# Softplus in one ScalarE instruction: a changed activation in the second layer of an attention and two-layer MLP kernel

## The chip, the cores and the metric

The kernel runs on one core of one Trainium2 chip. Its engines have queues of their own and wait for each other by semaphores: TensorE (PE, matmuls into PSUM; PEld is its weight load), VectorE (DVE), ScalarE (ACT), GpSimd (POOL) and SyncE (SP, which issues the transfers). The metric is the device time of one execution, in microseconds. The kernel before takes 1000.08 us, the median of three runs (998.30, 1000.08 and 1001.85).

## The reference, cut to what matters

Masked attention gives x (2304 tokens by 512), layer 1 is a gated unit behind an RMS norm, and layer 2, which the change touches, is an MLP with a softplus:

```python
def _moe2_ref(x, w_in, w_out):            # x (2304, 512), w_in (512, 2048), w_out (2048, 512)
    h = x @ w_in
    g = np.maximum(h, 0.0) + np.log1p(np.exp(-np.abs(h)))
    return (g @ w_out).astype(np.float32)
```

The weights arrive as 64-bit floats.

## The kernel before, in words

Every matmul operand is held as two parts, a rounded high part and the rest as a low part (xh and xl, gh and gl, and the two halves of each weight buffer). `mm3` (L255) does a product in three matmuls: high by high, high by low, low by high (L261).

The tokens lie in five chunks (`CUTS`: four of 512 and one of 256). Layer 1 has 12 blocks of 128 features, layer 2 has 16; a block is called f, and two of them make a group. There are four weight buffers (wa, w1, w2, w3; block f has the one of number f % 4), so the weights of the next group are read and split while the present group runs. `split` (L227) takes one tile of 512 columns: a DMA on SP, Abs on ScalarE that reads the upper words (L240), the sign mask (L241) and the assembly (L243) on VectorE, the rounding by a Copy on ScalarE (L246), two more steps on VectorE (L247, L249) and two on GpSimd (L252, L253). Its scratch tiles cvt, cvu and cvr exist once, so the next tile's Abs waits for L253 of the tile before. A block of layer 2 has two such tiles.

In layer 2 one block and one chunk go so: `project` gives h (128 features by the chunk's tokens) in one PSUM bank by 12 matmuls; `chain2` (L560) makes the softplus of h and splits it into gh and gl; `out2` (L581) multiplies them by the output weights, six matmuls of 512 columns for each 128 tokens and pair of blocks, and VectorE adds the bank to acc (L601; L599 the first time). The loop at L691 asks for the projections and chains of both blocks for chunk c, and only then for `out2` of chunk c-1. TensorE takes its matmuls in just this order; `out1` of layer 1's last chunk comes after the first projections of layer 2.

The other engines' order is not that of the text. `Program.emit` (L73) plans the whole of both layers with a cost for each operation (the helpers at L176 to L189) and a due time that follows from when TensorE needs the result; each engine takes, of what is ready by the plan, what is due first. The order is then fixed: on the chip every engine works its queue in order and waits at its head.

Activation functions come from table sets. The program loads one by name with `table` (L188), and an instruction that is marked as needing the table stays behind that load; Abs and Copy are not marked. One load stands ahead of layer 2 (L673), for the set that has Exp and Ln.

`chain2` takes three scratch tiles from the ring "ri" of six (four quarters of ssq, which layer 1 has no more use for, and two gv tiles), and a gh and a gl tile, of which there are four each.

Of the kernel before, what the change touches and what calls it, by code (L numbers as in the profile page):

```python
# [13 lines left out]
AF = mybir.ActivationFunctionType  # L14
ALU = mybir.AluOpType
AX = mybir.AxisListType
EXP_LN = "natural_log_exp_and_others"
# [25 lines left out]


class Program:
    """Instructions in program order, with what each reads and writes. emit() gives every
    engine a queue in which no instruction waits long while a later one could run. TensorE
    takes its main stream in program order, and the side stream where that one would wait."""

    def __init__(self):  # L50
        self.nodes, self.seen, self.ends = [], {}, []
# [103 lines left out]
def attn_glu_softplus(  # L155
# [14 lines left out]
    nc = tc.nc  # L170
    pr = Program()

    def all_of(key):
        return (key, 0, 1 << 30)

    def dve(n, fn, r, w, fast=False):  # L176
        pr.add("DVE", 69 + n / (1.92 if fast else 0.96), fn, r, w)

    def act(n, fn, r, w, table=False):
        pr.add("ACT", 93 + n / 1.2, fn, r + ([all_of("table")] if table else []), w)  # L180

    def pool(n, fn, r, w):
        pr.add("POOL", 110 + n * 2.2, fn, r, w)

    def dma(kb, fn, r, w):
        pr.add("SP", 650, fn, r, w, lag=1800 + 6 * kb)

    def table(name):  # L188
        pr.add("ACT", 1300, lambda: nc.scalar.preload_act_table_set(name), [], [all_of("table")])  # L189
# [10 lines left out]
    def ring(pool_, name, n, shape, dt=F32):  # L200
        return Ring([pool_.tile(shape, dt, name=f"{name}{i}") for i in range(n)], name)
# [18 lines left out]
    fk = {"gv": ring(const, "gv", 1, [128, CH]), "gh": ring(const, "gh", 2, [128, CH], F32R),  # L220
          "gl": ring(const, "gl", 2, [128, CH], F32R)}
# [288 lines left out]
    def project(f, o, c, ring_):  # L510
        pb, kb_ = ring_.next()
        pairs = []
        for kk, mv in enumerate(xs_of(c)):
            rx = [cols("xh", kk, CUTS[c], CUTS[c + 1]), cols("xl", kk, CUTS[c], CUTS[c + 1])]
            rw = wreg(f, o + kk * 128, 128)
            pairs.append((w_of(f, o + kk * 128), mv, lambda a, b, rx=rx, rw=rw: [rw[a], rx[b]]))
        n = CUTS[c + 1] - CUTS[c]
        pb = pb[:, :n]
        mm3(pb, kb_, pairs, n)
        return pb, kb_  # L520
# [39 lines left out]
    def chain2(f, c, hb, fk):  # L560
        h, kp = hb
        n = CUTS[c + 1] - CUTS[c]
        (e, ke), (l, kl), (t, kt) = (fk["ri"].next() for _ in range(3))
        e, l, t = e[:, :n], l[:, :n], t[:, :n]
        act(n, lambda: nc.scalar.activation(e, h, AF.Abs), [kp], [ke])  # L565
        act(n, lambda: nc.scalar.activation(e, e, AF.Exp, scale=-1.0), [ke], [ke], True)
        act(n, lambda: nc.scalar.activation(l, e, AF.Ln, bias=1.0), [ke], [kl], True)
        dve(n, lambda: nc.vector.tensor_scalar(out=t, in0=e, scalar1=1.0, scalar2=1.0,  # L568
                                               op0=ALU.add, op1=ALU.subtract), [ke], [kt], True)
        pool(n, lambda: nc.gpsimd.tensor_sub(t, e, t), [ke, kt], [kt])  # L570
        pool(n, lambda: nc.gpsimd.tensor_add(l, l, t), [kl, kt], [kl])  # L571
        dve(n, lambda: nc.vector.scalar_tensor_tensor(out=l, in0=h, scalar=0.0, in1=l,  # L572
                                                      op0=ALU.max, op1=ALU.add), [kp, kl], [kl])
        sh, kh = fk["gh"].next()
        sl, ksl = fk["gl"].next()
        sh, sl = sh[:, :n], sl[:, :n]
        dve(n, lambda: nc.vector.tensor_copy(sh, l), [kl], [kh], True)  # L577
        dve(n, lambda: nc.vector.tensor_sub(sl, l, sh.bitcast(F32)), [kl, kh], [ksl])  # L578
        return f, (sh, sl), (kh, ksl)

# [25 lines left out]
    def weights(f, wpool):  # L606
        w_t[f] = (wpool, f"w{f % 4}")
        for s in range(3 if f < W1N else 2):
            split(wpool, f"w{f % 4}", f, s)

    with tc.manual_schedule():
        table(EXP_LN)
        pr.add("DVE", 200, lambda: nc.vector.memset(ones, -1.0 / DM), [], [all_of("ones")])
        pr.add("DVE", 100, lambda: nc.vector.memset(eps, 1e-6), [], [all_of("eps")])
        pr.add("DVE", 100, lambda: nc.vector.memset(lnc, math.log(RC)), [], [all_of("eps")])
        wa = const.tile([128, 2, 1536], F32R, name="wa")
        first = {}

        plan = {}

        def at_step(u, fn, *args):
            plan.setdefault(u, []).append((fn, args))

        at_step(8, weights, 0, wa)
        g0 = {}

        def half(c, o):
            first[c, o] = project(0, o, c, f_banks)

        def glu(c):  # L630
            table("silu_and_others")
            g0[c] = chain1(0, c, first[c, 0], first[c, 512], fk)
            table(EXP_LN)

        for c, u in enumerate(START):
            at_step(u, stats, c, f_banks)
            at_step(u + 2, half, c, 0)
            at_step(u + 3, half, c, 512)
            if c < 2:
                at_step(u + 4, glu, c)  # L640

        def fill(u):
            pr.side = True
            for fn, args in plan.pop(u, ()):
                fn(*args)
            pr.side = False

        dma(96, lambda: nc.sync.dma_start(out=pat[64:128], in_=mk), [], [all_of("pat")])
        dma(64, lambda: nc.sync.dma_start(out=id_sb, in_=ident), [], [all_of("id")])
        dma(2, lambda: nc.sync.dma_start(out=rg_sb, in_=rg), [], [all_of("rg")])  # L650
        for i in range(WARM):
            pr.add("PE", 400, lambda: nc.tensor.matmul(
                f_banks.t[0][:, :128], lhsT=ones, rhs=ones, start=True, stop=True), [all_of("ones")], [("bank6", 0, 128)])
        at_stack = ExitStack()
        attention(at_stack, fill)
        pr.emit()
        at_stack.close()
        wb = ctx.enter_context(tc.tile_pool(name="wb", bufs=1))
        acc = wb.tile([128, KD * NT], F32, name="acc")
        acc_t = acc.rearrange("p (k t) -> p k t", k=KD)  # L660
        acc_o = acc.rearrange("p (i n) -> p i n", n=DM)
        wts = [wa] + [wb.tile([128, 2, 1536], F32R, name=f"w{i}") for i in range(1, 4)]
        for key, dt in (("gv", F32), ("gh", F32R), ("gl", F32R)):
            for i in range(EXTRA[key]):
                fk[key].t.append(wb.tile([128, CH], dt, name=f"{key}x{i}"))
        fk["ri"] = Ring([ssq[:, i * CH:(i + 1) * CH] for i in range(NT // CH)] + fk["gv"].t, "ri")
        todo = []
        for gi, fs in enumerate(groups):
            for f in fs:
                if f:  # L670
                    weights(f, wts[f % 4])
            if gi == len(G1):
                table(EXP_LN)  # L673
            if gi == 0:
                out1(0, 0, [g0[0]])
                stats(3, banks)
                stats(4, banks)
                banks.k += 2
                table("silu_and_others")
                gate, val = first[2, 0], first[2, 512]  # L680
                for c in range(2, NCH):
                    todo.append((out1, 0, c, [chain1(0, c, gate, val, fk)]))
                    if c < NCH - 1:
                        gate, val = project(0, 0, c + 1, banks), project(0, 512, c + 1, banks)
                    if c == 2:
                        out1(0, 1, [g0[1]])
                    elif c > 2:
                        fn, *args = todo.pop(0)
                        fn(*args)
                continue  # L690
            for c in range(NCH):  # L691
                if gi < len(G1):
                    gt = [chain1(f, c, project(f, 0, c, banks), project(f, 512, c, banks), fk) for f in fs]
                    todo.append((out1, gi, c, gt))
                else:
                    st = [chain2(f, c, project(f, 0, c, banks), fk) for f in fs]
                    todo.append((out2, gi, c, st))
                while len(todo) > 1:
                    fn, *args = todo.pop(0)
                    fn(*args)  # L700
        for fn, *args in todo:
            fn(*args)
        pr.emit(start=0)
# [67 lines left out]
```

## Time and profile before

| | profiled execution |
|---|---|
| span of the profiled execution (its own time, first to last instruction) | 994.3 us |
| median of the three runs | 1000.08 us |
| TensorE busy | 938.9 us, 94% |
| VectorE busy | 740.4 us, 74% |
| ScalarE busy | 377.1 us, 38% |
| GpSimd busy | 611.0 us, 61% |
| DMA, mean rate | 59 GB/s |

The span leaves out what lies around the instructions, 5.8 us against the median. A matmul's busy time (0.39 us for 512 columns) overlaps with that of the next one, so TensorE can show as busy while it advances slowly; the distance from one start to the next shows its pace. PEclk is the TensorE clock that was granted, 1.00 being 2.4 GHz. Attention ends at about 125 us, layer 1 runs to about 556, layer 2 to the end; the two overlap a little.

### The profile page before, as it was taken

To read this page: it belongs to the slowest core of one execution; us is meant where nothing else is said; L and a number is where in the kernel's file an instruction comes from. 1 tells how busy PE (TensorE), PEld (TensorE's weight loads), DVE (VectorE), ACT (ScalarE), POOL (GpSimd) and SP (SyncE) were. 2 spreads that over 40 slices of the span, in tenths; PEclk is the share of its full clock that TensorE was granted. 3 is DMA by queue.
4 is the path that set the end of the run, shared out by engine and by line. 5 is a ranking of instruction groups with operands and counts; after the bars stand their busy time and mean duration, and the time that the engine had idled before them with its cause. 6 is when DMAs were issued, how large, how long until landed. Compare 5 with 4: busy or idle time off the path is not lost.

```text
span 994.3 us, 14313 instructions
## 1 busy us (share of the span) xinstructions
PE 938.9 (94%) x5412; PEld 774.4 (78%) x5412; DVE 740.4 (74%) x1214; ACT 377.1 (38%) x689; POOL 611.0 (61%) x502
## 2 busy tenths in 40 slices
PE   6788899999999999999999999989899999999998
PEld 5667678888888888888888877777777778777787
DVE  5787798876674574574743788998889897989776
ACT  4676843322231231221333534334334433433332
POOL 2555666676573573573756965766766667657453
PEclk8988999999999999999999989999999999999999
DMA  9995222222120120110100011101101010110013
GB/s 196 222 208 112 94 61 66 64 67 82 43 64 22 43 64 22 43 64 22 64 22 1 22 42 44 43 22 43 43 22 64 22 63 23 43 43 1 1 74 117
DMA packets 17846, 59.09 MB, mean 59 GB/s; under 512 B 2353, under 2 KB 3057, under 8 KB 17777
## 3 DMA queue, kind: packets, MB, share of 16 engines
q1 hardware_dynamic: 17776, 58.18, 21.0%
q8 instruction: 42, 0.69, 0.3%
q14 instruction: 28, 0.22, 0.1%
HBM read 53.45 MB, written 4.72 MB: 59 GB/s over the span
## 4 chain that ended last, share of the span: by engine, by line
PE 57%; DVE 20%; POOL 10%; issue 8%; DMA 2%; ACT 2%; SPq 0%; POOLq 0%; DVEq 0%; ACTq 0%
PE bank L261 52%; DVE acc L601 3%; POOL cvt L252 2%; DVE cvt L243 2%; POOL gv L571 2%; POOL ssq L571 2%; DVE gl L578 2%; PE bank L431 2%; PE bank L363 2%; POOL w L253 1%; DVE glx L578 1%; DVE gv L572 1%; PE bank L407 1%; DMA rg_sb<-rms_g 1%; DVE gvx L568 1%
## 5 line engine op out<-in xcount | busy, mean ns | idle before, releaser
L261 PE MATMUL bank<-xh,w 128*128 128x512 f32 (+1 forms) x1200 | 350.1, 368 | 0.0
L261 PEld LDWEIGHTS bank<-xh,w 128*128 128x128 f32 x1200 | 218.6, 188 | 37.6
L261 PE MATMUL bank<-xl,w 128*128 128x512 f32 (+1 forms) x600 | 220.7, 368 | 0.0
L261 PEld LDWEIGHTS bank<-xl,w 128*128 128x128 f32 x600 | 113.1, 189 | 19.0
L261 PE MATMUL bank<-xh,wa 128*128 128x512 f32 (+1 forms) x400 | 120.5, 372 | 1.5 <-DVE gv L531 1.2
L570 POOL TENSOR_TENSOR ssq<-ssq 128x512 f32<-128x512 f32 (+1 forms) x40 | 49.7, 1243 | 113.1 <-DVE ssq L568 110.0
L252 POOL TENSOR_TENSOR cvt<-cvt,w 128x512 f32<-128x512 f32 x51 | 80.0, 1569 | 42.5 <-ACT w L246 29.0
L601 DVE TENSOR_TENSOR acc<-bank,acc 128x512 f32<-128x512 f32 x126 | 85.4, 681 | 26.2 <-PE bank L261 26.1
L240 ACT ACTIVATE cvt<-raw 128x512 f32<-128x512 f32 x68 | 45.7, 672 | 153.3 <-POOL w L253 132.7
L553 DVE TENSOR_TENSOR acc<-bank,acc 128x512 f32<-128x512 f32 (+1 forms) x120 | 73.0, 630 | 20.4 <-PE bank L261 20.2
L243 DVE SCALAR_TENSOR_TENSOR cvt<-cvt,cvu 128x512 uint32<-128x512 uint32 x68 | 64.6, 950 | 29.2 <-ACT cvt L240 28.5
L261 PEld LDWEIGHTS bank<-xh,wa 128*128 128x128 f32 x400 | 72.9, 189 | 15.7 <-DVE gv L531 2.4
L565 ACT ACTIVATE ssq<-bank 128x512 f32<-128x512 f32 (+1 forms) x80 | 43.8, 547 | 95.5 <-PE bank L261 95.5
L261 PE MATMUL bank<-w,ghx 128*128 128x512 f32 x224 | 70.2, 394 | 6.7 <-DVE ghx L577 5.9
L261 PE MATMUL bank<-xl,wa 128*128 128x512 f32 (+1 forms) x200 | 74.3, 372 | 0.0
L253 POOL TENSOR_TENSOR w<-cvt,cvr 128x512 fp32r<-128x512 f32 x51 | 67.7, 1328 | 9.8 <-DVE cvr L249 8.1
L261 PE MATMUL bank<-w,gh 128*128 128x512 f32 x208 | 66.5, 401 | 6.6 <-DVE gh L577 5.9
L530 POOL TENSOR_TENSOR gv<-gv,ssq 128x512 f32<-128x512 f32 (+1 forms) x31 | 36.8, 1187 | 46.8 <-ACT gv L529 46.8
L249 DVE SCALAR_TENSOR_TENSOR cvr<-raw,cvu 128x512 f32<-128x512 uint32 x68 | 59.4, 874 | 3.7
L261 PE MATMUL bank<-ghx,w 128*128 128x512 f32 (+1 forms) x192 | 57.3, 362 | 0.0
L571 POOL TENSOR_TENSOR gv<-gv,gvx 128x512 f32<-128x512 f32 (+1 forms) x40 | 55.3, 1382 | 2.0
L261 PEld LDWEIGHTS bank<-w,ghx 128*128 128x128 f32 x224 | 41.3, 188 | 18.2 <-DVE ghx L577 8.8
(119 smaller groups left out, 1957.1 us busy)
## 6 DMA issues: line engine op xcount, KB each, us to landing
raw<-w SPq DMA_DIRECT2D x68, 512.0 KB, 3.5
out<-acc SPq DMA_DIRECT2D x18, 256.0 KB, 2.0
vb<-v_loc SPq DMA_DIRECT2D x8, 432.0 KB, 11.6
vb<-v_str SPq DMA_DIRECT2D x8, 384.0 KB, 12.3
kl<-k_loc SPq DMA_DIRECT2D x7, 432.0 KB, 11.0
qs<-q_t SPq DMA_DIRECT2D x8, 304.0 KB, 12.0
ks<-k_str SPq DMA_DIRECT2D x8, 297.0 KB, 12.5
ql<-q_t SPq DMA_DIRECT2D x7, 304.0 KB, 12.1
```

The costliest lines, as they stand in the source:

```text
L240: act(512, lambda: nc.scalar.activation(t, whi.bitcast(F32), AF.Abs, scale=2.0 ** -112), [kraw], [kt])
L243: dve(512, lambda: nc.vector.scalar_tensor_tensor(out=t.bitcast(U32), in0=t.bitcast(U32), scalar=3, in1=u, op0=ALU.logical_shift_left, op1 ...
L249: dve(512, lambda: nc.vector.scalar_tensor_tensor(out=r, in0=wlo, scalar=2.0 ** -52, in1=u.bitcast(F32), op0=ALU.mult, op1=ALU.mult), [kra ...
L252: pool(512, lambda: nc.gpsimd.tensor_sub(t, t, hi.bitcast(F32)), [kt, khi], [kt])
L253: pool(512, lambda: nc.gpsimd.tensor_add(lo, t, r), [kt, kr], [klo])
L261: lambda a=a, b=b, i=i, st=st, mv=mv: nc.tensor.matmul(o, lhsT=st[a], rhs=mv[b], start=(first and i == 0), stop=(last and i == m - 1)),
L530: pool(n, lambda: nc.gpsimd.tensor_mul(a, a, r), [ka, kr], [ka])
L553: dve(n, lambda a=a, pb=pb: nc.vector.tensor_add(a, pb, a), [kp, ka], [ka])
L565: act(n, lambda: nc.scalar.activation(e, h, AF.Abs), [kp], [ke])
L570: pool(n, lambda: nc.gpsimd.tensor_sub(t, e, t), [ke, kt], [kt])
L571: pool(n, lambda: nc.gpsimd.tensor_add(l, l, t), [kl, kt], [kl])
L601: dve(DM, lambda a=a, pb=pb: nc.vector.tensor_add(a, pb, a), [kp, ka], [ka])
```

## The change

`chain2` computes the softplus by one ScalarE instruction that reads the bank in PSUM, and rounds the high part by a Copy on ScalarE in place of the cast on VectorE. The low part is still a subtraction on VectorE. Abs, Exp, Ln, the rounding correction (L568, L570), the sum (L571) and the maximum (L572) go. One scratch tile is taken and not three. The table load ahead of layer 2 names another set. Four lines of a comment become empty, so that the line numbers of the rest above `chain2` stay.

```diff
     def chain2(f, c, hb, fk):
         h, kp = hb
         n = CUTS[c + 1] - CUTS[c]
-        (e, ke), (l, kl), (t, kt) = (fk["ri"].next() for _ in range(3))
-        e, l, t = e[:, :n], l[:, :n], t[:, :n]
-        act(n, lambda: nc.scalar.activation(e, h, AF.Abs), [kp], [ke])
-        act(n, lambda: nc.scalar.activation(e, e, AF.Exp, scale=-1.0), [ke], [ke], True)
-        act(n, lambda: nc.scalar.activation(l, e, AF.Ln, bias=1.0), [ke], [kl], True)
-        dve(n, lambda: nc.vector.tensor_scalar(out=t, in0=e, scalar1=1.0, scalar2=1.0,
-                                               op0=ALU.add, op1=ALU.subtract), [ke], [kt], True)
-        pool(n, lambda: nc.gpsimd.tensor_sub(t, e, t), [ke, kt], [kt])
-        pool(n, lambda: nc.gpsimd.tensor_add(l, l, t), [kl, kt], [kl])
-        dve(n, lambda: nc.vector.scalar_tensor_tensor(out=l, in0=h, scalar=0.0, in1=l,
-                                                      op0=ALU.max, op1=ALU.add), [kp, kl], [kl])
+        l, kl = fk["ri"].next()
+        l = l[:, :n]
+        act(n, lambda: nc.scalar.activation(l, h, AF.Softplus), [kp], [kl], True)
         sh, kh = fk["gh"].next()
         sl, ksl = fk["gl"].next()
         sh, sl = sh[:, :n], sl[:, :n]
-        dve(n, lambda: nc.vector.tensor_copy(sh, l), [kl], [kh], True)
+        act(n, lambda: nc.scalar.activation(sh, l, AF.Copy), [kl], [kh])
         dve(n, lambda: nc.vector.tensor_sub(sl, l, sh.bitcast(F32)), [kl, kh], [ksl])
         return f, (sh, sl), (kh, ksl)
...
             if gi == len(G1):
-                table(EXP_LN)
+                table("softplus")
```

## Rows read from the trace of the kernel before

**Rows 1.** Windows: length, busy us (count) of PE, PEld, DVE, ACT, POOL; clock, DMA.
```profile
300.00:350.00 50.00, 50.00 (x256) 42.82 (x256) 24.55 (x40) 11.71 (x20) 23.86 (x21) 1.00 0.10 32
700.00:750.00 50.00, 46.42 (x210) 36.97 (x209) 43.83 (x71) 18.74 (x34) 32.11 (x26) 1.00 0.10 35
```
**Rows 2.** Timeline of TensorE: start, length, what, count, idle before.
```profile
546.27 0.40 PE L261 MATMUL bank<-xh,w 128*128 128x256 f32 x2
...
546.63 0.40 PE L261 MATMUL bank<-xh,w 128*128 128x256 f32 x2
...
555.82 0.39 PE L261 MATMUL bank<-xh,wa 128*128 128x512 f32 x1
...
700.60 0.62 PE L261 MATMUL bank<-xh,wa 128*128 128x512 f32 x2
...
701.28 0.62 PE L261 MATMUL bank<-xh,wa 128*128 128x512 f32 x2
...
990.10 0.39 PE L261 MATMUL bank<-w,glx 128*128 128x512 f32 x1
```
**Rows 3.** Chain of waits, 555 to the end: start, length, what.
```profile
600.37 1.42 POOL ssq L570
...
872.82 1.42 POOL ssq L570
```
**Rows 4.** Windows in the change of layers.
```profile
575.00:580.00 5.00, 4.75 (x11) 3.78 (x12) 2.71 (x5) 0.63 (x1) 4.63 (x5) 0.50 0.00 0
```
**Rows 5.** Timeline of TensorE at a stall.
```profile
707.80 0.73 PE L261 MATMUL bank<-w,gh 128*128 128x512 f32 x2 [1.97 <-DVE gh L577]
709.00 0.50 PE L261 MATMUL bank<-w,gl 128*128 128x512 f32 x1 [0.47 <-DVE gl L578]
```
**Rows 6.** Timeline of VectorE at that stall.
```profile
707.00 0.41 DVE L247 TENSOR_SCALAR cvu<-cvt 128x512 uint32<-128x512 uint32 x1
707.33 0.41 DVE L577 CAST gh<-gv 128x512 fp32r<-128x512 f32 x1
...
708.27 0.68 DVE L578 TENSOR_TENSOR gl<-gv,gh 128x512 fp32r<-128x512 f32 x1
```
**Rows 7.** Timeline of all engines: one chain in the last group.
```profile
962.72 0.39 PE L261 MATMUL bank<-xh,w 128*128 128x512 f32 x1
...
963.20 0.60 ACT L565 ACTIVATE ssq<-bank 128x512 f32<-128x512 f32 x1 [0.79 <-PE bank L261]
...
963.83 0.63 ACT L566 ACTIVATE ssq<-ssq 128x512 f32<-128x512 f32 x1
...
964.50 0.63 ACT L567 ACTIVATE gv<-ssq 128x512 f32<-128x512 f32 x1
...
965.11 0.42 DVE L568 TENSOR_SCALAR gvx<-ssq 128x512 f32<-128x512 f32 x1
...
966.99 1.35 POOL L571 TENSOR_TENSOR gv<-gv,gvx 128x512 f32<-128x512 f32 x1
...
970.46 0.69 DVE L578 TENSOR_TENSOR glx<-gv,ghx 128x512 fp32r<-128x512 f32 x1
...
973.82 0.62 PE L261 MATMUL bank<-w,ghx 128*128 128x512 f32 x2
```
**Rows 8.** Timeline of ScalarE around the last table load.
```profile
550.13 1.28 ACT L189 ACT_TABLE_LOAD   x1
551.43 0.42 ACT L535 ACTIVATE ghx<-gvx 128x256 fp32r<-128x256 f32 x1
...
552.79 0.63 ACT L556 ACTIVATE xh<-acc 128x512 fp32r<-128x512 f32 x1
```
**Rows 9.** Lines by themselves: count, ns min/median/max, first and last start.
```profile
L240 ACT ACTIVATE cvt<-raw x26: 667/680/691, 562.6 to 911.5; 128x512 f32<-128x512 f32 x26
...
L189 ACT ACT_TABLE_LOAD  x7: 1283/1283/1283, 0.7 to 550.1; - x7
```
**Rows 10.** Waits, 600 to 900: us in total, times, longest.
```profile
ACT cvt L240 <- POOL w L253: 65.2, 16, 6.5
```

## The prediction, made before the changed kernel ran

> **What bounds the kernel now.** I read the table of 50 us windows first. In layer 1 (300 to 350 us) TensorE is busy all of the 50 us at a granted clock of 1.00 and VectorE for 24.6; in layer 2 (700 to 750) TensorE falls to 46.4 at the same clock while VectorE stands at 43.8 and GpSimd at 32.1 [rows 1]. So layer 1 is bound by TensorE alone, and in layer 2 TensorE sometimes waits. Busy shares understate these waits, since matmuls overlap: the time to the next one is the better measure.
>
> That is read in the TensorE timeline. Undisturbed, a pattern of three 512-column matmuls starts again after 0.68 us (700.60 to 701.28), 0.2267 each; three of 256 columns take 0.36 (546.27 to 546.63), 0.120 each [rows 2]. From the code, one chunk of 512 tokens and one feature block f costs layer 2 12 projection matmuls and 12 of the output projection, all 512 wide; the last chunk (256 tokens) costs 12 of 256 and 6 of 512. A group (two blocks, five chunks) is thus 2 x (4 x 24 + 6) = 204 wide and 24 narrow ones: 204 x 0.2267 + 24 x 0.120 = 49.1 us. The chain of waits shows the real period: the same L570 instruction comes back six times from 600.37 to 872.82 us, five groups in 272.45 us, 54.5 each [rows 3]. So 5.35 us of every group are stalls.
>
> The sum over all of layer 2: its first matmul starts at 555.82, the last of the program at 990.10 [rows 2], which with that one's own 0.23 is 434.5 us. The work between is 8 groups (1632 wide, 192 narrow) and 24 narrow ones of layer 1's last output chunk: 1632 x 0.2267 + 216 x 0.120 = 395.9 us. The difference, **38.6 us, is all that TensorE loses from there to the end**. Five groups account for 26.8 of it; the rest, 11.8, lies mostly in the change of layers, where TensorE stands still around 570 and then, after that idle time, runs at a granted clock of 0.50 (1.2 of 2.4 GHz) in 575 to 580 [rows 4], 11 matmuls in 5 us where 22 fit: some 2.5 us of the loss is that clock.
>
> Who causes a stall: at 707.80 TensorE has waited 1.97 us for VectorE's L577, at 709.00 another 0.47 for L578 [rows 5]. VectorE at that moment alternates steps of a weight split (L247) with the steps of the activation [rows 6]. The activation chain is simply too long for its due time.
>
> **How long the chain may be, and is.** TensorE's order is projection of both blocks for chunk c, output of chunk c-1, both projections for c+1, output of c. The second block's chain therefore has one output chunk and two projections: from 962.72 + 0.23 to 973.82, 10.9 us [rows 7]. After a chunk 0 it is less, since the output chunk before it is the short one (12 matmuls): 24 x 0.2267 + 12 x 0.2267 = 8.2 us; after chunk 3 it is 24 x 0.2267 + 24 x 0.120 = 8.3. Today's chain without any weight split beside it runs from 963.20 to 970.46 + 0.69 = 971.15, 8.2 us after TensorE finished [rows 7]. It just fits; with the splits of the next weights (four a group, three VectorE operations apiece behind the sign mask) between its steps it doesn't. That is the stall.
>
> **The change, part by part.**
> - Removed: per chain two ScalarE operations (Exp, Ln: 0.63 each), one fast VectorE operation (L568, 0.42), two on GpSimd (about 1.35 each, one of them shown), L572 and the L577 rounding on VectorE (not shown in the rows; like the L578 beside them they are single 512-column passes, and I use 0.69 as their upper end) [rows 7]. None of it is on TensorE, so its worth is only the stalls. VectorE, 43.8 of 50 and so 47.7 a group of 54.5, loses 0.42 + 0.69 + 0.69 = 1.8 in each of eight chains and about 1.0 in the two short ones: 16.4, which leaves 31 of 49.1. GpSimd, 32.1 of 50 and so 35.0, loses 8 x 2.7 + 2 x 1.4 = 24.4 and keeps 11.
> - Softplus from PSUM: no row shows it. Nearest is Abs of the same bank tile, 0.60; the table functions Exp and Ln take 0.63; two passes would be 1.26 [rows 7]. I take 0.60 and keep 0.60 to 1.26 as ends.
> - Copy to the rounded high part: 0.63, as L556, which writes the same type from the same shape [rows 8]. The subtraction stays: 0.69 [rows 7].
> - The new chain: 0.60 + 0.63 + 0.69 = 1.9, with handovers of up to 0.1 as between the rows of the old one about 2.3 us; 2.9 at the far end. Against a limit of 8.2 that leaves about 6 us (at worst 5.3) for whatever stands ahead of it in the ScalarE and VectorE queues. VectorE's queue holds at most a split step or an accumulation, each 0.4 to 0.7.
> - Scratch: one tile of the ring of six a chain in place of three, so tiles come back later than they are needed; nothing waits more. The PSUM bank is released by ScalarE's first pass and no longer by VectorE's seventh step, which can only help.
> - Table loads: the program places the seven that there are, 1.283 us each [rows 9]; the last, at 550.13, is followed by a Copy at 551.43, without a gap [rows 8]. The new set is called after one function alone, the two old ones "..._and_others". Weight splits go on with Abs (L240) in layer 2: 26 times from 555 on [rows 9]. If that set doesn't serve Abs, a load stands before each Abs and another before the next Softplus: 0 to 26 x 2 x 1.283 = 67 us of ScalarE, spread over 435. I take the upper end. ScalarE then has per group 8 x 1.23 + 2 x 0.8 for the chains (a 256-column Copy takes 0.42 [rows 8]), 4 x 1.31 for the splits, 8 x 1.283 for loads: 27 of 49.1 us. On one chain a pair of loads and the Abs is 2 x 1.283 + 0.68 = 3.2 us, within the 6 left. So I cost them at nothing; their cover is this slack, and each us beyond it would be a us of TensorE, four times a group.
>
> The Trainium skill, "ScalarE: Activation LUTs", section "Table sets: the hidden batching unit", says that cheap functions such as copy and abs are in every set; by that there are no added loads, and two rivals below lose their ground, ScalarE as the bound and most of the slower one. The rows bear it out for the two sets in use, under which Abs and Copy run with no load but the seven; for the new set no row shows it, so both rivals keep a chance. Its section "What ACT_TABLE_LOAD costs" puts a drain of 1.38 us beside the 1.283, 2.66 in all; the rows above show 1.283 and no gap on either side, so the measurement decides (by the page, the pair of loads would be 5.3 us and use up the slack).
>
> **The sum.** Without the stalls TensorE is the bound, as it is in layer 1, where a chain of six operations on three engines with the same due times leaves it busy for 50 of 50 us [rows 1]. No gain is possible beneath that: 994.3 - 38.6 = 955.7 us of span. I keep 1 us for a remainder in the change of layers, where loads, four Copies of layer 1's result and the first Softplus meet on ScalarE: 956.7. The span is 5.8 below the median of the runs, 1000.08 (998.3 to 1001.85): **962.5 us**, 3.8% faster. Those runs differ by 0.36%, so I count under 0.3%, some 3 us, as no change.
>
> **Rivals.**
> - *Part of the stalls stays.* VectorE keeps 31 us of a group, splits and accumulations above all, and the subtraction, alone at the chain's end, can stand behind them; the layer change still has a table load, Copies and accumulations in one place. For it: the stalls now fall where split steps interleave [rows 6]. Against: what is left in front of one subtraction is two or three steps, under 2 us, with 6 to spare. If half of the groups' loss stays (2.7 x 6 = 16): 978 us.
> - *ScalarE becomes the bound through table loads.* If the set holds Softplus alone and Copy needs another too, each chain has two loads: 20 a group and up to 4 more for the splits, 24 x 1.283 = 31 us beside 16.7 of work: 47.5 of 49.1. With its in-order waits I give such a group the 54.5 us it has today: about 1000 us, no change. Only the name of the set speaks for it.
> - *Slower: ScalarE's queue is held by a weight split.* Abs waits for GpSimd's L253 of the split before; 16 such waits in 600 to 900 us add up to 65.2, the longest 6.5 [rows 10]. Today the activation's first operation is behind it too, but afterwards all but one of its operations are on this engine. A wait of 6.5, a pair of loads and the Abs (3.2) and the chain (2.3) make 12.0, which is 3.8 over a due time of 8.2 and 1.1 over 10.9. With two of four splits at each, a group loses 9.8 where it lost 5.35: 26 splits are 6.5 groups, x 4.45 = 29, with the layer change as now 1029 us. It decides from a mean wait of about 5 us in front of a Softplus that is ready. Against it: these waits come from a GpSimd that is behind by its activation work (L570, L571), and all of that goes; and ScalarE's idle time before Abs costs nothing while no Softplus is ready.
> - *A Softplus of two passes* (1.26) changes nothing in the sum.
>
> **Chances.** Forecast 0.79; part of the stalls stays 0.12; ScalarE bound 0.04; slower 0.05. Range 959 to 976: below it only the 955.7 floor and the runs' spread of some 2 us reach; above it I leave out the last two cases and half of the second. Faster by over 0.3%: 0.91; within: 0.04; slower: 0.05.
>
> **What would show it.** Right: windows of layer 2 with TensorE busy for 50 of 50 us at 1.00; a group period near 49.1 in place of 54.5; no wait of TensorE on L577's successor or the subtraction; no fall of the clock near 575; VectorE near 32 of 50, GpSimd near 11. Loads: up to about 54 added lines of table loads beside Abs, with TensorE undisturbed beside them. Wrong: TensorE waiting for ScalarE or for the subtraction more than once a group; a Softplus above 1.3 us; a matmul interval that differs from 0.2267.

## The result, and the profile after

| | before | after |
|---|---|---|
| median of the runs | 999.56 us (4 runs, 998.30 to 1001.85) | 957.64 us (4 runs, 955.64 to 958.67) |
| span of the profiled execution | 994.3 us | 955.8 us |
| TensorE / VectorE / ScalarE / GpSimd busy | 938.9 / 740.4 / 377.1 / 611.0 us | 926.0 / 597.4 / 401.1 / 411.7 us |

The changed kernel is faster by 4.2%: ratio 0.9585, interval 0.9563 to 0.9608. The forecast was 962.5 us with a range from 959 to 976; the measured time lies 1.4 us below the range.

Where the time came from, the windows of the kernel after show (length, busy us and count of PE, PEld, DVE, ACT, POOL, granted clock, DMA). They answer to [rows 1] and [rows 4]; the last two are as long as one group of layer 2.

```profile
300.00:350.00 50.00, 50.00 (x256) 42.86 (x255) 24.51 (x40) 11.72 (x20) 23.92 (x21) 1.00 0.11 32
...
575.00:580.00 5.00, 5.00 (x24) 4.14 (x23) 4.55 (x7) 0.88 (x2) 2.58 (x2) 1.00 0.28 89
...
700.00:750.00 50.00, 50.00 (x233) 41.90 (x232) 30.35 (x46) 27.44 (x38) 11.11 (x8) 1.00 0.13 43
...
600.00:649.10 49.10, 49.10 (x230) 41.14 (x229) 29.46 (x45) 26.55 (x37) 11.07 (x9) 1.00 0.13 43
649.10:698.20 49.10, 49.10 (x230) 41.12 (x229) 29.45 (x45) 26.55 (x37) 11.08 (x9) 1.00 0.13 43
```

Layer 1 is as it was. In layer 2 TensorE begins 233 matmuls in 50 us where it began 210. The first projections of four groups in a row start at 605.09, 654.23, 703.37 and 752.51, 49.14 us apart, which is what a group's matmuls need. The clock no longer falls at 575. The chain of waits, from 540 us to the end, is one unbroken run of matmuls (start, length, what):

```profile
539.95 411.33 PE bank L261 x1938
951.28 0.02 issue
951.31 1.37 DVE acc L593 x2
```

Its two ends for layer 2, which answer to the first and last matmul in [rows 2], in the timeline of TensorE:

```profile
555.77 0.39 PE L261 MATMUL bank<-xh,wa 128*128 128x512 f32 x1
...
951.56 0.39 PE L261 MATMUL bank<-w,glx 128*128 128x512 f32 x1
```

From 555.77 to 951.56 + 0.23 are 396.0 us, against 434.5 before: 38.5 less, and 0.1 from the 395.9 that were worked out. The medians differ by 41.9 us. Of the rest, 0.3 lies around the span (next section); that the other 3 are chance ahead of layer 2 is likely, but not shown: beside the experiments below the difference was about 40.

The new chain in ScalarE's timeline, which answers to [rows 7]:

```profile
698.95 1.28 ACT L240 ACT_TABLE_LOAD   x1
700.25 0.67 ACT L240 ACTIVATE cvt<-raw 128x512 f32<-128x512 f32 x1
700.94 1.28 ACT L565 ACT_TABLE_LOAD   x1
706.29 0.60 ACT L565 ACTIVATE ssq<-bank 128x512 f32<-128x512 f32 x1 [4.07 <-PE bank L261]
706.92 0.63 ACT L569 ACTIVATE ghx<-ssq 128x512 fp32r<-128x512 f32 x1
```

and its last step on VectorE, then, in TensorE's timeline, the matmul that first uses this chunk's parts:

```profile
707.58 0.69 DVE L570 TENSOR_TENSOR glx<-ssq,ghx 128x512 fp32r<-128x512 f32 x1 [2.87 <-ACT ghx L569]
```
```profile
716.97 0.62 PE L261 MATMUL bank<-w,ghx 128*128 128x512 f32 x2
```

Softplus takes 0.60 us, the chain 706.29 to 708.27, 2.0 us, and it is ready 8.7 us before it is used. Over the 49 chains of 512 tokens in 600 to 900 us, the time from the end of the last projection matmul to the end of the subtraction is 2.0 to 5.7 us (median 2.7). In the kernel before it is 8.5 to 14.8 (44 chains, median 12.9). When TensorE never waits, as here, it comes to the low part of a chain 9.1 to 13.9 us after that projection, so 21 of the 44 old chains have under 0.2 us to spare or none, and the new ones at least 6.4. The table loads came, as the upper end had them. From ScalarE's lines:

```profile
L240 ACT ACT_TABLE_LOAD x26 | 33.4, 1283 | 0.5
L565 ACT ACT_TABLE_LOAD x26 | 33.4, 1283 | 0.5
...
L189 ACT ACT_TABLE_LOAD x7 | 9.0, 1283 | 0.8 <-PEq L752 0.7
```

One stands before each Abs of a weight split and one before the next Softplus, 52 beside the program's seven, and none beside a Copy.

### The profile page after: what moved, and what is told of

It reads as the page before. It is cut to its first block, busy times and chain, and to the rows that moved or that the text cites. A ratio compares the mean times of both kernels' runs of the same rounds, so it can differ in the third digit from the quotient of the medians.

```text
span 955.8 us, 13823 instructions
## 1 busy us (share of the span) xinstructions
PE 926.0 (97%) x5412; PEld 777.2 (81%) x5412; DVE 597.4 (62%) x974; ACT 401.1 (42%) x661; POOL 411.7 (43%) x342
## 4 chain that ended last, share of the span: by engine, by line
PE 88%; DVE 4%; DMA 3%; issue 2%; ACT 1%; POOL 1%; SPq 0%; DVEq 0%; POOLq 0%; ACTq 0%
PE bank L261 84%; DMA rg_sb<-rms_g 1%; DMA vb<-v_loc 1%; PE bank L431 1%; PE bank L363 1%; DMA ql<-q_t 1%; PE bank L407 1%; DVE xl L464 1%; DVE mz L379 0%; DVE ssq L283 0%; POOL cvt L252 0%; DVE mz L375 0%; DVE mz L380 0%; PE bank L276 0%; DVE sm L282 0%
## 5 line engine op out<-in xcount | busy, mean ns | idle before, releaser
L243 DVE SCALAR_TENSOR_TENSOR cvt<-cvt,cvu 128x512 uint32<-128x512 uint32 x68 | 56.0, 823 | 68.9 <-ACT cvt L240 67.6
L252 POOL TENSOR_TENSOR cvt<-cvt,wa 128x512 f32<-128x512 f32 x17 | 23.2, 1365 | 105.9 <-ACT wa L246 65.2
L565 ACT ACTIVATE ssq<-bank 128x512 f32<-128x512 f32 (+1 forms) x54 | 29.7, 550 | 90.9 <-PE bank L261 90.7
L261 PE MATMUL bank<-w,gh 128*128 128x512 f32 x208 | 64.2, 389 | 0.0
L246 ACT ACTIVATE w<-cvt 128x512 fp32r<-128x512 f32 x51 | 32.2, 632 | 59.2 <-DVE cvt L243 30.9
L261 PE MATMUL bank<-gh,w 128*128 128x512 f32 (+1 forms) x168 | 54.1, 374 | 0.0
## 6 DMA issues: line engine op xcount, KB each, us to landing
vb<-v_loc SPq DMA_DIRECT2D x8, 432.0 KB, 11.0
kl<-k_loc SPq DMA_DIRECT2D x7, 432.0 KB, 10.8
```

What stands on the lines that cost most here:

```text
L243: dve(512, lambda: nc.vector.scalar_tensor_tensor(out=t.bitcast(U32), in0=t.bitcast(U32), scalar=3, in1=u, op0=ALU.logical_shift_left, op1 ...
L246: act(512, lambda: nc.scalar.activation(hi, t, AF.Copy), [kt], [khi])
L252: pool(512, lambda: nc.gpsimd.tensor_sub(t, t, hi.bitcast(F32)), [kt, khi], [kt])
L261: lambda a=a, b=b, i=i, st=st, mv=mv: nc.tensor.matmul(o, lhsT=st[a], rhs=mv[b], start=(first and i == 0), stop=(last and i == m - 1)),
L565: act(n, lambda: nc.scalar.activation(l, h, AF.Softplus), [kp], [kl], True)
```

## The experiments

All times are medians; each ratio is to runs of the kernel before on the same chip, whose medians were 997.0 to 998.7 us.

**What lies between span and time.** The kernel before, unchanged.

> The kernel before, unchanged. Open point: the prediction added 5.8 us between the profiled span (994.3) and the median (1000.08); the changed kernel shows 957.64 - 955.8 = 1.8 us. Theory 1: what lies around the span is 1.8 us in both kernels, and the profiled execution of before was merely a short one of a spread of some 4 us; then each execution here has its time 1.7 to 1.9 us above its own span, and spans run from 994 to 1000 with a median near 997.7. Theory 2: the kernel before has more around its span, and each time is about 5 us above its span, spans near 994. If theory 1 holds, the granted clock or the start of the program should differ between executions.

Measured: 997.39 us (12 runs, 995.90 to 1001.37), ratio 0.9997 (0.9980 to 1.0013). Each run has its time 2.1 us above its own span: 995.90 with 993.8, 997.41 with 995.3, 1001.37 with 999.3. So theory 1 holds, with 2.1 for this kernel and 1.8 for the changed one (957.64 with 955.8, 955.64 with 953.9). Over all 70 executions of the unchanged kernel beside the experiments, the median is 997.66 us and the spans go from 992.0 to 1001.8. Where executions differ is seen in the timeline of its TensorE:

```profile
556.80 0.39 PE L261 MATMUL bank<-xh,wa 128*128 128x512 f32 x1
...
991.12 0.39 PE L261 MATMUL bank<-w,glx 128*128 128x512 f32 x1
```

Layer 2 takes 434.3 us from first to last start, as in [rows 2] (555.82 to 990.10); only its begin moved by 1.0 us. In a run of the next experiment it begins at 560.37. The last matmul of attention (L431) starts at 122.4 us in the first profile, 123.3 in this one and 126.9 in that run, and layer 2 begins 433.4 to 433.5 us later in all three: the spread arises in attention. The granted clock differs there, in the first 50 us above all (windows of the unchanged kernel, then of its first profile); that it is the cause is not shown.

```profile
0.00:50.00 50.00, 34.40 (x513) 29.94 (x513) 33.44 (x87) 26.07 (x59) 18.32 (x29) 0.80 0.99 206
```
```profile
0.00:50.00 50.00, 34.54 (x519) 29.98 (x521) 34.18 (x89) 26.72 (x61) 18.27 (x29) 0.88 0.98 209
```

**What the table loads cost.** One word of the weight split changed; the sign bit that Abs removed is shifted out by the next step.

```diff
-nc.scalar.activation(t, whi.bitcast(F32), AF.Abs, scale=2.0 ** -112)
+nc.scalar.activation(t, whi.bitcast(F32), AF.Copy, scale=2.0 ** -112)
```

> The changed kernel with Abs in the weight split replaced by Copy with the same scale (the sign bit is shifted out in the next step), so that no table load is needed in the second layer. Theory 1 (loads lie in ScalarE's idle time): the 52 loads beside Abs and Softplus vanish, ScalarE loses 67 us of busy time, and the time is that of the changed kernel within 0.3% (957.6, ratio to before 0.958). Theory 2 (loads still cost something on the path): 3 to 10 us less.

Measured: 957.55 us, ratio 0.9582 (0.9558 to 0.9606). ScalarE falls from 27.4 to 16.1 us of 50, only the seven loads are left, and the time is that of the changed kernel. The 52 loads cost ScalarE 66.7 us and the kernel nothing that can be measured.

```profile
700.00:750.00 50.00, 50.00 (x238) 42.04 (x237) 30.09 (x45) 16.07 (x28) 11.11 (x8) 1.00 0.13 43
```

**Which part of the change counts.** Two instructions in the old table set in place of Softplus; then Softplus with the rounding left on VectorE; then the rounding alone moved.

```diff
-act(n, lambda: nc.scalar.activation(l, h, AF.Softplus), [kp], [kl], True)
+act(n, lambda: nc.scalar.activation(l, h, AF.Exp), [kp], [kl], True)
+act(n, lambda: nc.scalar.activation(l, l, AF.Ln, bias=1.0), [kl], [kl], True)
...
-                table("softplus")
+                table(EXP_LN)
```

> The changed kernel with the softplus as two ScalarE instructions, Exp from PSUM and Ln of 1 + that, in the old table set, in place of one Softplus. Theory 1 (anything that stays on ScalarE alone is short enough): chain about 3 us, no added table loads, TensorE busy throughout layer 2, time equal to the changed kernel within 0.3% (957.6). Theory 2 (it is the single instruction that counts): some stalls come back, time 965 or more.

Measured: 958.17 us, ratio 0.9598 (0.9573 to 0.9623): the same time, without an added table load.

```diff
-act(n, lambda: nc.scalar.activation(sh, l, AF.Copy), [kl], [kh])
+dve(n, lambda: nc.vector.tensor_copy(sh, l), [kl], [kh], True)
```

> The changed kernel with the rounding left on VectorE: one Softplus, a cast and a subtraction, about 2 us of chain; VectorE at 36 us a group. Theory 1: all of the gain is in the single instruction, 957.6 within 0.3%. Theory 2 (the rounding on ScalarE is needed too, since the cast queues behind the split on VectorE): 962 to 975.

Measured: 957.33 us, ratio 0.9607 (0.9583 to 0.9632), with VectorE at 34.1 us of 50. The Copy on ScalarE adds nothing to it. Alone, in the kernel before (the same two lines the other way round):

> The kernel before, with the high part rounded on ScalarE as in the change and all else as it was: 5 of 47.7 us a group leave VectorE, the chain keeps its nine steps and its 8.2 us. Theory 1 (latency): most of the stalls stay, 985 to 998. Theory 2 (VectorE's throughput): with a tenth of its load gone the larger part of the stalls goes too, 962 to 980.

Measured: 993.10 us, ratio 0.9961 (0.9944 to 0.9978), a gain of 0.4%; layer 2 takes 432.0 us in place of 434.3. The chains still take 7.1 to 15.3 us. VectorE has 41.6 us of 50 in place of 43.8, and TensorE begins 211 matmuls in place of 210:

```profile
700.00:750.00 50.00, 46.84 (x211) 37.12 (x210) 41.55 (x59) 26.08 (x47) 34.29 (x26) 1.00 0.13 43
```

Its waits of TensorE in 600 to 900 us (us in total, times, longest) are still those of the chain's last two steps:

```profile
PE bank L261 <- ACT gh L577: 5.1, 4, 1.6
PE bank L261 <- ACT ghx L577: 4.0, 4, 1.6
PE bank L261 <- DVE gl L578: 3.3, 5, 1.0
PE bank L261 <- DVE glx L578: 2.1, 3, 1.0
```

So taking 2 us of 50 off VectorE does not end the stalls while the chain is long.

**A long chain without VectorE's work.** The changed kernel without Abs gets its chain lengthened behind Softplus.

```diff
 act(n, lambda: nc.scalar.activation(l, h, AF.Softplus), [kp], [kl], True)
+t, kt = fk["ri"].next()
+t = t[:, :n]
+pool(n, lambda: nc.gpsimd.tensor_add(t, l, l), [kl], [kt])
+pool(n, lambda: nc.gpsimd.tensor_sub(l, t, l), [kl, kt], [kl])
```

> As the padded chain before, but with the two GpSimd operations alone: chain about 5 us, 3 under the shortest due time of 8.2 us; GpSimd at about 35 us a group as in the kernel before. Theory 1: no stalls, 957.6 within 0.4%; with the longer pad at 982 the edge lies between 5 and 7.6 us. Rival: it is GpSimd's presence on VectorE's and ScalarE's queues that costs, then it lies near the longer pad, 970 to 985.

Measured: 958.21 us, ratio 0.9611 (0.9578 to 0.9643); no stall in the groups, with GpSimd at 35.9 us of 50, more than the 32.1 of [rows 1]:

```profile
700.00:750.00 50.00, 50.00 (x233) 41.89 (x232) 35.18 (x45) 16.03 (x28) 35.93 (x31) 1.00 0.13 43
```

The same with four Copies in place on ScalarE behind that:

> The changed kernel without Abs, its chain made long again without VectorE: after Softplus two GpSimd operations (l + l, then minus l, which gives l back; 2.7 us) and four Copies in place on ScalarE (2.5 us), so a chain of about 7.6 us; per group GpSimd about 35 us, ScalarE about 42, VectorE 31. Theory 1 (latency against a due time of 8.2 to 10.9 us): the margin is gone, stalls of 1 to 4 us a group return at chunks 0 and 3 and beside splits, 965 to 985. Theory 2 (VectorE's throughput): no stalls, 957.6 within 0.3%.

Measured: 982.26 us, ratio 0.9847 (0.9821 to 0.9873). The stalls are back although VectorE has 33.7 us of 50, and TensorE waits for the chain's last step (windows, then the waits of TensorE in 600 to 900, then one chain: its last projection matmul, its subtraction and the matmul that waits for it):

```profile
700.00:750.00 50.00, 47.48 (x219) 38.90 (x219) 33.69 (x42) 34.58 (x65) 35.42 (x28) 1.00 0.10 34
```
```profile
PE bank L261 <- DVE gl L578: 7.6, 6, 1.5
PE bank L261 <- DVE glx L578: 6.6, 5, 1.5
```
```profile
754.29 0.39 PE L261 MATMUL bank<-xh,w 128*128 128x512 f32 x1
...
763.57 1.71 DVE L578 TENSOR_TENSOR gl<-ssq,gh 128x512 fp32r<-128x512 f32 x1 [2.12 <-ACT gh L577]
...
765.33 0.50 PE L261 MATMUL bank<-w,gl 128*128 128x512 f32 x1 [1.01 <-DVE gl L578]
```

The 5 and 7.6 us of the expectations leave out the waits in the queues. Measured as above, the chain of five operations takes 5.4 to 10.8 us (median 7.1), is at least 1.4 us early, and is free; the one of nine takes 9.0 to 12.9 (median 10.7) and costs 24 us. So a long chain brings stalls without VectorE's load. ScalarE's load rose with it, from 16.0 to 34.6 us of 50, and no run has that load beside a short chain.

**VectorE's work without the long chain.** Two subtractions that nobody reads, behind each chain.

```diff
+for _ in range(2):
+    t, kt = fk["ri"].next()
+    t = t[:, :n]
+    dve(n, lambda t=t: nc.vector.tensor_sub(t, l, sh.bitcast(F32)), [kl, kh], [kt])
```

> The changed kernel without Abs, with two more VectorE subtractions for each chain whose result nobody reads: VectorE at about 43 us of a group, as in the kernel before with the rounding on ScalarE, but behind the chain and not in it. Theory now: below TensorE's 49.1 us VectorE's load costs next to nothing while the chain is short, 957.6 within 0.5%. Rival: VectorE's load by itself brings the stalls, through later accumulations and splits, 970 to 990.

Measured: 957.65 us, ratio 0.9587 (0.9561 to 0.9613). VectorE has 42.2 us of 50, more than with the rounding moved alone (41.6), the chains take 2.0 to 4.7 us, and there is no stall:

```profile
700.00:750.00 50.00, 50.00 (x234) 41.87 (x233) 42.24 (x67) 16.19 (x28) 12.10 (x8) 1.00 0.13 43
```

**More time for the old chain.** If a due time too near were all, the old chain would do with a later one. The first build:

```diff
-                while len(todo) > 1:
+                while len(todo) > (1 if gi < len(G1) else 2):
```

> The kernel before with its old chain, but in layer 2 TensorE does the output of chunk c-2 after the projections of chunk c, in place of chunk c-1: the chain gets one more output chunk and two projections (about 10.9 us) before it is due. Theory 1 (latency: the chain of 8 us and more was due in 8.2 to 10.9 us): the stalls of the groups vanish with nothing taken off any engine, group period about 49.1 us, time 962 to 970. Theory 2 (throughput: VectorE at 47.7 us of work a group, slowed beside GpSimd, can't go faster): the stalls return, spread otherwise, and the time stays at 990 to 1002.

Measured: 1294.48 us, ratio 1.2965 (1.2935 to 1.2994). With four gh and four gl tiles, the chain of chunk c writes the tiles that the output of chunk c-2 reads, and stands ahead of it: the output computes with the wrong chunk and waits for a chain that has only begun. It became a test of no lead at all. TensorE waits in 600 to 900:

```profile
PE bank L261 <- DVE ghx L577: 41.3, 15, 7.5
PE bank L261 <- DVE gh L577: 39.3, 14, 7.5
```

Layer 2 takes 734.1 us in place of 434.3, which is 7.5 us for each of the 40 pairs of chains; part of it comes through the granted clock, whose mean over the span is 0.878. The second build has six tiles of each; for their room cvr is written over cvu, and the norm's scratch shares a tile with layer 1's activation, without an order between the two uses, so layer 1 computes wrong numbers, but with the same instructions:

```diff
-EXTRA = {"gv": 1, "gh": 2, "gl": 2}
+EXTRA = {"gv": 1, "gh": 4, "gl": 4}
```

> The lag of two again, now with six gh and six gl tiles, so that the chain of chunk c no longer writes the tiles that the output of chunk c-2 reads (room for them: the weight split writes cvr over cvu, the small scratch of the norm moves). Old chain, nothing taken off any engine. Theory 1 (latency, due time): the group stalls of 5.35 us vanish, groups take about 49.1 us, time 958 to 968. Theory 2 (throughput: VectorE at 47.7 us a group is the bound in effect): the stalls come back elsewhere, time 988 to 1000.

Measured: 1020.34 us, ratio 1.0232 (1.0216 to 1.0248). TensorE now waits for the step that frees the chain's bank:

```profile
PE bank L260 <- DVE gv L572: 23.8, 6, 4.4
PE bank L260 <- DVE ssq L572: 8.4, 5, 1.7
```

The third gives the projections and the output four banks each (and orders the shared scratch):

```diff
+h_banks, o_banks = Ring(banks.t[:4], "bank"), Ring(banks.t[4:], "bank", 4)
...
-                    st = [chain2(f, c, project(f, 0, c, banks), fk) for f in fs]
+                    st = [chain2(f, c, project(f, 0, c, h_banks), fk) for f in fs]
```

> The lag of two, third build: the run before showed TensorE waiting for L572, the step of the old chain that frees its PSUM bank, which has a due time of its own in the ring of eight. Now the projections of layer 2 have four banks and the output four others, so that neither the bank nor gh and gl of a chain is due before another 10.9 us have passed; no work is taken off any engine. Theory 1 (latency against due time): group stalls go, period about 49.1 us, 957 to 970. Theory 2 (the throughput of VectorE beside GpSimd): stalls come back with yet another releaser, 985 to 1020.

Measured: 998.74 us, ratio 1.0012 (0.9996 to 1.0028). A later due time for the chain alone gains nothing here. TensorE no longer waits for the chain in 600 to 900 us; it waits for accumulations (L602), and VectorE is busy for 51.6 of 54.3 us (windows of two groups, then TensorE's waits in 600 to 900):

```profile
655.78:710.07 54.29, 50.77 (x229) 42.25 (x229) 51.61 (x75) 21.14 (x38) 37.37 (x29) 0.97 0.12 39
710.07:763.50 53.43, 50.94 (x228) 42.33 (x228) 50.76 (x73) 21.14 (x38) 36.52 (x29) 0.97 0.12 40
```
```profile
PE bank L261 <- DVE acc L602: 15.7, 5, 3.5
```

So VectorE's work, over 50 us a group here, is itself above TensorE's 49.1. But the build changes two more things. From the last matmul of attention to layer 2 it takes 437.6 us in place of 433.4, which hides that layer 2 became shorter (431.5 in place of 434.3). And with four output banks in turn TensorE returns to a bank 9.4 us after its last matmul, where the ring of eight gives about 12 (an estimate from the order of the matmuls at 0.2267 each), while the accumulation begins 6.7 us after it (median in 600 to 900) and not 1.6 as in the kernel before. Whether VectorE's load or the earlier due time of these banks holds this build was not separated.

With the rounding moved to ScalarE as well:

> The old chain with both reliefs at once: the lag of two with banks of their own for projection and output (998.7 us alone, VectorE at 51.2 us of a group of 53.9), and the rounding on ScalarE (993.1 alone, VectorE at 41.4 of 50). Theory now: the kernel before had two bounds close together, the chain's due time and VectorE's work of 48 to 51 us a group against TensorE's 49.1; lifting one alone leaves the other. Then VectorE has about 46 us a group here, stalls go, 958 to 972. Rival: something else holds it (GpSimd at 37 a group, the banks), 985 to 1000.

Measured: 984.39 us, ratio 0.9861 (0.9834 to 0.9888): more than either alone (0.4% and nothing), and less than expected. One group, and TensorE's waits in 600 to 900:

```profile
715.00:767.50 52.50, 50.00 (x229) 40.91 (x229) 45.74 (x65) 26.36 (x48) 37.30 (x29) 1.00 0.12 41
```
```profile
PE bank L261 <- DVE acc L602: 10.2, 13, 1.0
```

Layer 2 takes 416.7 us. VectorE has 45.7 of 52.5 us and TensorE still waits for accumulations in its queue, which begin 6.2 us (median) after their bank's last matmul. So VectorE's load by itself does not explain what is left. That the accumulations stand behind steps of the old chain which wait for GpSimd, or that four banks are too few, is possible, but only argued; a build that gives them another place in the queue, or more banks, was not tried.

## Why the prediction was right and where it was wrong

- **The failed step is the last term of the sum**: "The span is 5.8 below the median of the runs, 1000.08". That 5.8 was taken as a fixed amount around the program. It is 2.1 for the kernel before and 1.8 for the changed one. The other 3.7 us are luck, as the executions differ in attention: the profiled one, with a time of its own of 994.3 + 2.1 = 996.4, was 1.3 below the 997.66 of the 70 executions beside the experiments, and the median of the three runs 2.4 above. The same sum with 1.8 gives 956.7 + 1.8 = 958.5, and the floor 955.7 + 1.8 = 957.5. The lower end of the range rested on the same term, so it was too high by as much.
- **The remainder of 1 us** for the change of layers was 0.1: layer 2 took 396.0 against 395.9. That the whole span also meets its floor (955.8 against 955.7) is luck, since both profiled executions happen to begin layer 2 at 555.8.
- **The loss of TensorE**, 38.6 us, was right: 38.5. So were the group (49.1), the clock at 575 (1.00) and the statement that TensorE is the bound afterwards.
- **The price of Softplus** (0.60, chain 2.3) was right: 0.60 and 2.0. **The table loads** were right in number (52) and in cost (nothing): without them the time is the same. The Trainium skill, "ScalarE: Activation LUTs", section "Table sets: the hidden batching unit", has abs in every set; the 26 loads before Abs differ from that for the set that is loaded here for Softplus. The drain of 1.38 us in its section "What ACT_TABLE_LOAD costs" does not show either: the Abs at 700.25 follows the load of 698.95 to 700.23 at once.
- **VectorE's and GpSimd's loads** were right: 30.4 of 50 us against 32, and 11.1 a group against 11.
- **"The activation chain is simply too long for its due time"** was right as the cause of the stalls, and the traces show it: 8.5 to 14.8 us of chain against 9.1 to 13.9. A long chain brings stalls with a free VectorE (982.26), and a busy VectorE brings none with a short chain (957.65). Whether it was the only limit is open: with a later due time the old chain gains nothing (998.74), with VectorE at over 50 us a group, but that build has its accumulations due earlier too. The change takes off both, the length and VectorE's work, so the forecast did not depend on it.
- **"VectorE's queue holds at most a split step or an accumulation, each 0.4 to 0.7"** was too low: some of its steps take up to 1.8 us beside GpSimd (last section). It did no harm, since the "about 6 us" left over were 6.4 at the least, with all waits.
- That one instruction replaces the seven ahead of the rounding is not what counts: two on one engine do as well (958.17).

## What to carry to other kernels

Between a profiled span and the median of other runs lies the spread of executions as well as a fixed remainder: use the remainder of runs that have both. When a tightly packed engine waits now and then, count its matmuls against the time they need to get the floor; a chain that passes between three engines has a due time for its result and another for its PSUM bank, and moving one of them, or taking a little off one engine alone, gained next to nothing here. Extra work on an engine with idle time in the right place, such as 67 us of table loads here, was free.

## What the runs showed of the hardware

Some VectorE steps cost more than twice as much at one time as at another, and others hardly vary (kernel before, 610 to 910 us; count, ns min/median/max, first and last start, shapes):

```profile
L568 DVE TENSOR_SCALAR gvx<-ssq x27: 286/917/1516, 621.1 to 904.7; 128x512 f32<-128x512 f32 x22, 128x256 f32<-128x256 f32 x5
...
L578 DVE TENSOR_TENSOR gl<-ssq,gh x14: 407/1182/1666, 614.5 to 895.7; 128x512 fp32r<-128x512 f32 x11, 128x256 fp32r<-128x256 f32 x3
...
L572 DVE SCALAR_TENSOR_TENSOR gv<-bank,gv x27: 409/678/693, 614.8 to 898.5; 128x512 f32<-128x512 f32 x21, 128x256 f32<-128x256 f32 x6
...
L601 DVE TENSOR_TENSOR acc<-bank,acc x94: 673/678/694, 631.7 to 910.0; 128x512 f32<-128x512 f32 x94
```

L568 and L578, which read SBUF alone, go up to 1516 and 1666 ns; L572 and L601, with one operand in PSUM, stay under 700. The timeline shows what the long ones have in common. Of the 512-column steps in these 300 us, all tile names taken together, the 22 of L568 that overlap in time with no GpSimd instruction take 412 to 431 ns, and the 22 that do overlap 896 to 1516; of L578, 15 take 677 to 693 and 28 take 1172 to 1668. L601 takes 673 to 694 either way. In the changed kernel (600 to 900 us) 41 of its subtractions (L570) run beside no GpSimd instruction and take 682 to 693, the 7 others 1589 to 1653. An overlap does not always cost: with the rounding alone moved, some of the overlapping L578 stay at 677.

The Trainium skill, "GPSIMD Engine Reference", section "Specifications", has GpSimd share its SBUF interfaces with VectorE, with contention for VectorE instructions in a 2-port mode or with two SBUF inputs; the rows fit that, but no run here took GpSimd away by itself.

So VectorE's load in one schedule does not carry over to another: it was 47.7 us a group in the kernel before, and the same steps came to 50.8 and 51.6 when the stalls moved elsewhere. With the durations that its steps have beside no GpSimd instruction (0.41 to 0.69 us for 512 columns) a group would be some 41 us, an estimate summed from this trace.
